# A planned one-core kernel (H3 mixer, then a token-mixing MLP): k by DMA transpose, x statistics from an early copy, tables and silu on GpSimd, PE transposes for three token groups, and an order read from a table

## The chip, the cores and the metric

One NeuronCore of a Trainium2 chip runs the whole program. The metric is device time of one execution in microseconds (us), the median of three runs. Engines: PE (TensorE, the matrix engine; PEld is its weight load), DVE (VectorE), ACT (ScalarE), POOL (GpSimd), SP (SyncE, which issues DMAs). SBUF is the on-chip memory, PSUM the accumulators that PE writes.

## The reference

Everything is bfloat16, sequence S = 2048, width D = 640, F = 1728. `sa ... gb` are six vectors of width D from `silu(c) @ w_mod`.

```python
h = layernorm(x) * (1 + ca) + sa                       # x is A_q
k_shift = sum_t k[s - t] * shift_k[:, t]               # 4 taps, causal
kv = k_shift * v
y  = irfft(rfft(kv, 2S) * rfft(ssm_k, 2S))[:S] + kv * ssm_D      # long convolution along s
x  = x + ga * (h * y)
h  = layernorm(x) * (1 + cb) + sb
t  = gelu(layernorm(h) @ w1)                           # D x D
x1 = h + shift_tokens(t) @ w2                          # four column groups shifted by 1, -1, 2, -2 tokens
x  = x + gb * (x1 + gelu(layernorm(x1) @ w3) @ w4)     # D x F, F x D
```

## The kernel before

**A planner sets the order.** The kernel first lists tasks with `add(engine, cost, function, reads, writes, prio)`: each is a few instructions for one engine, or for whichever of two engines would end earlier. `Planner.run` then plays the list through with the written costs, the dependencies that follow from the named SBUF regions, and four PSUM slots; among ready tasks of an engine the smaller `prio` goes first. The instructions are emitted in the order of the planned starts. On the chip each engine works through its own queue in that order, and semaphores hold an instruction until its inputs are there; a DMA waits likewise in SP's or POOL's queue.

**Stages.** The long convolution is a transform of length 4096 done with matrix products.

- Tables. Sines for the products are made on the chip: POOL writes integer ramps (`iota`, L312), DVE turns them into angles (two `tensor_scalar`, L323 and L324, on 512 columns), ACT takes the sine (L331). `Gs` in RG serves the forward transform, `Hs` in RH the inverse, `F1bd` the first stage.
- Loads. `ssm_k` goes to Ra, two pieces issued by SP and three by POOL. k goes to R3 as it lies (`ktok`, L255, issued by POOL) and is turned with k_transpose: 80 PE transposes into PSUM and twelve copies into kT (in R5). v is turned on the way by four DMA transposes issued by SP (L258) into vT (in R5).
- Forward transform of ssm_k: DVE 32x32 block transposes from Ra to Rb (L386, each behind a one-column add L442), `stage1` on PE (L399) with casts of PSUM into T01 by ACT or DVE (L229, L231), `stage2` on PE (L418) with casts into R3. Between them `k_shift` (L474, PE) with DVE's product with v (L480).
- Forward transform of kv: transposes into Ra (`kvL`), the same two stages, results in R5 (`XS`). Six `mod` pieces (L507) make the vectors.
- x is loaded into Ra, now free (L543, four DMAs in token order for the end of the kernel). DVE takes statistics of each of 16 tiles of 128 tokens (`ln1_stats`, L569 and L570), POOL makes scale and bias (`ln1_fin`, L575 to L578; the power is a GpSimd operation), and `make_q` applies them on ACT (L584) and DVE (L588, L589).
- `inverse1`, ten pieces: DVE multiplies the two transforms (L608, and L610 with a copy whose halves are swapped by DMA, L603), PE multiplies by `EA`, `EB` (L619, L620). Then `inverse2` on PE (L648) with casts into `y_all` (Rb).
- The MLP, in eight groups of two tiles: `chain_a` (L707, L710: y times q, added to x), sum of squares on ACT (L699), mean and power on POOL (`ln_finish`, L685 to L694), `chain_b` (L721 to L723: h), again squares and POOL, `chain_c` (L732), a DMA transpose by SP (L734), `mm_w1` (L764, L774; gelu on ACT, L766, L780), `mm_w2` (L819, sum on DVE L827), a third layernorm (L837 on ACT) with a DMA transpose (L839), `mm_w3` (L854, gelu), `mm_w4` (L877), three DVE operations (L883, L888, L889) and the output DMAs (L892).

The transposition of a tile for w1 reads

```python
add("DVE", 0.42, lambda e, hn=hn, A=A, i=i: nc.vector.tensor_scalar(hn, h_all[:, A, :], rn[0][:, i:i + 1], rn[1][:, i:i + 1], ALU.mult, ALU.add),
    r=[hk_(A), rn[2]], w=[hk], prio=prio)
add("SP", 1.25, lambda e, hn=hn, i=i: nc.sync.dma_start_transpose(hT[:, :, i * P:(i + 1) * P], hn), r=[hk], w=[hTk + ("t",)], prio=prio, lat=1.6)
```

Of the kernel before, what the change touches and what calls it, by code (L numbers as in the profile page):

```python
# [8 lines left out]
BF = mybir.dt.bfloat16  # L9
F32 = mybir.dt.float32  # L10
# [28 lines left out]
class Planner:  # L41
# [3 lines left out]
    SEM = {"PE": 0.22, "ACT": 0.12, "DVE": 0.10, "POOL": 0.15, "SP": 0.0}  # L45
# [44 lines left out]
    def run(self):  # L90
# [4 lines left out]
        order = []  # L95

# [11 lines left out]
        while todo:  # L108
# [49 lines left out]
def kernel(  # L158
# [34 lines left out]
    ident = modv[:, 4, 0:P]  # L193
# [6 lines left out]
    ktok = R3[:, 10240:20480].rearrange("p (t d) -> p t d", d=D)  # L200
# [15 lines left out]
    def ca(n):  # L216
        return 0.12 + 0.00083 * n

    def cd(n):
        return 0.08 + 0.00105 * n  # L220

    def dma(eng, kb, fn, r=(), w=(), prio=None):
        q = nc.sync if eng == "SP" else nc.gpsimd
        return add(eng, 0.55 if eng == "SP" else 1.0, lambda e, q=q, fn=fn: fn(q), r, w, prio, lat=2.0 + kb / 280.0)
# [25 lines left out]
    for b in range(ND):  # L250
        add("SP" if b < 2 else "POOL", 1.5 if b < 2 else 1.0, lambda e, b=b: (nc.sync if b < 2 else nc.gpsimd).dma_start(sT[:, b, :], A_ssm_k[b * P:(b + 1) * P, :]),
            w=[("Ra", 2048 * b, 2048 * b + 2048)], lat=3.5 + 1.5 * b)
    dma("POOL", 8, lambda q: q.dma_start(skT[:], A_shift_k.rearrange("(b p) j -> p b j", p=P)), w=[("skT", 0, 1)])
    for sc in range(4):
        add("POOL", 1.0, lambda e, sc=sc: nc.gpsimd.dma_start(ktok[:, 4 * sc:4 * sc + 4, :], k_flat[512 * sc:512 * sc + 512, :].rearrange("(t p) d -> p t d", p=P)),  # L255
            w=[("R3", 10240 + 2560 * sc, 12800 + 2560 * sc)], lat=9.0 + 2.5 * sc)
    for sc in range(4):
        add("SP", 5.8, lambda e, sc=sc: nc.sync.dma_start_transpose(vT[:, :, sc * 512:(sc + 1) * 512], v_flat[sc * 512:(sc + 1) * 512, :]),  # L258
            w=[("vT", 5 * sc, 5 * sc + 5)], lat=1.5)
# [10 lines left out]
    s64 = mem.tile([P, 1], F32, name="s64")  # L270
    pci = mem.tile([P, 2], I32, name="pci")
# [12 lines left out]
    add("POOL", 0.3, lambda e: nc.gpsimd.memset(F1bd[:], 0.0), w=[("F1", 0, 1)], prio=-2)  # L284
    add("POOL", 0.6, lambda e: make_identity(nc, ident), w=[("modB", 5, 6)], prio=5)

    def f(e):
# [4 lines left out]
        nc.vector.tensor_copy(s64[:], pci[:, 1:2])  # L292
    add("DVE", 0.7, f, r=[("pidx", 0, 1)], w=[("scol", 0, 1)], prio=-2)

    gcol = mem.tile([P, 2, 4], F32, name="gcol")
    hcol = mem.tile([P, 2, 4], F32, name="hcol")
    ci = mem.tile([P, 4], I32, name="ci")

    def f(e):
        nc.gpsimd.iota(ci[:], pattern=[[16, 4]], base=0, channel_multiplier=0)  # L300
    add("POOL", 0.2, f, w=[("ci", 0, 1)], prio=-3)

    def f(e):
        for col, s_ in ((gcol, s64), (hcol, s32o)):
            nc.vector.tensor_scalar(col[:, 0, :], ci[:], s_[:], None, ALU.mult)
            nc.vector.tensor_scalar(col[:, 1, :], ci[:], s_[:], 2048.0, ALU.mult, ALU.add)
    add("DVE", 0.5, f, r=[("ci", 0, 1), ("scol", 0, 1)], w=[("cols", 0, 1)], prio=-1)
    tmp = {"R3": R3[:].bitcast(I32), "RK": RK[:].bitcast(I32)}

    def itab(reg, o, n, pattern, base, prio):  # L310
        ti = tmp[reg][:, o:o + n]
        add("POOL", 0.2 + 0.0012 * n, lambda e: nc.gpsimd.iota(ti, pattern=pattern, base=base, channel_multiplier=0),  # L312
            w=[(reg, 2 * o, 2 * o + 2 * n)], prio=prio)
        return ti, (reg, 2 * o, 2 * o + 2 * n)

    def angles(it, reg, o, s_col, cs_col, ss_col, q, prio):
        ti, tk = it
        n = ti.shape[1]
        ms, ma = (tmp[reg][:, o + n * i:o + n * (i + 1)] for i in range(2))
        keys = [(reg, 2 * o + 2 * n * i, 2 * o + 2 * n * (i + 1)) for i in range(2)]  # L320
        for m_, k_, col in ((ms, keys[0], ss_col), (ma, keys[1], cs_col)):
            def f(e, m_=m_, col=col):
                nc.vector.tensor_scalar(m_, ti, s_col, col, ALU.mult, ALU.add)  # L323
                nc.vector.tensor_single_scalar(m_, m_, q - 1, ALU.bitwise_and)  # L324
            add("DVE", 0.2 + 0.0013 * n, f, r=[tk, ("cols", 0, 1), ("scol", 0, 1)], w=[k_], prio=prio)
        return ms, ma, keys

    def sin_to(dst, ms, q, n, r, w, prio, neg=False):
        b = (b_neg if neg else b_pos)[dst.start_partition():dst.start_partition() + dst.shape[0], :]
        sc = (2.0 if neg else -2.0) * PI_LO / q  # L330
        add("ACT", 0.2 + 0.00098 * n, lambda e: nc.scalar.activation(dst, ms, ACT.Sin, scale=sc, bias=b),  # L331
            r=[r, ("consts", 0, 1)], w=[w], prio=prio)

    it = itab("R3", 4608, 32, [[2, 32]], 1, -2)
    ms, ma, ky = angles(it, "R3", 4640, s32[:], 32.0, 0.0, 128, -1)
    for q in range(4):
        sl = slice(32 * q, 32 * q + 32)
        sin_to(F1bd[sl, q, 0, :], ma[sl, :], 128, 32, ky[1], ("F1", 0, 1, "f"), -1)
        sin_to(F1bd[sl, q, 1, :], ms[sl, :], 128, 32, ky[0], ("F1", 0, 1, "f"), -1, True)
    it = itab("R3", 0, 512, [[2, 8], [128, 64]], 1, -1)  # L340
    for kb in range(4):
        ms, ma, ky = angles(it, "R3", 512 + 1024 * kb, s64[:], gcol[:, 1, kb:kb + 1], gcol[:, 0, kb:kb + 1], 8192, -1)
        k2s = slice(8 * kb, 8 * kb + 8)
        ms3, ma3 = (t.rearrange("p (a b) -> p a b", a=8) for t in (ms, ma))
        wk = ("RG", 2048 * kb, 2048 * kb + 2048, "g")
        sin_to(Gs[:, k2s, 0, 0, :], ma3, 8192, 512, ky[1], wk, 0)
        sin_to(Gs[:, k2s, 0, 1, :], ms3, 8192, 512, ky[0], wk, 0, True)
        sin_to(Gs[:, k2s, 1, 0, :], ms3, 8192, 512, ky[0], wk, 0)
        sin_to(Gs[:, k2s, 1, 1, :], ma3, 8192, 512, ky[1], wk, 0)
# [5 lines left out]
    it = itab("RK", 1536, 64, [[1, 64]], 0, 8)  # L355
    ms, ma, ky = angles(it, "RK", 1600, s64[:], 16.0, 0.0, 64, 30)
# [127 lines left out]
    for j in range(12):  # L484
        k_transpose(j, 20 + (j - 2) / 3.0)
# [483 lines left out]
```

## Time and profile before

| | |
|---|---|
| median of three runs | 370.57 us (369.43 to 371.05) |
| profiled execution | 368.94 us, of which 367.2 from its first to its last instruction (the span) |
| mean granted PE clock in it | 0.916 of full |
| moved by DMA | 35.08 MB |

The profile is one execution. Its lines give for a group of instructions: source line, engine, operation, output<-input, count, then busy us and mean ns of one, then the idle time of the engine just before them and what ended it. Buffer names drop their numbers, so R is R3 or R5 and T is T01. In lines by stretch, each engine's busy us stands with its instruction count in brackets, then the granted PE clock, the DMA share and GB/s. Lines of the chain that ended last give start, length and what. SPq is SP issuing a DMA.

### The profile page before, as it was taken

Reading aid. Unit: us, or ns where it says so; the run is one execution under the profiler, and the core shown is the slowest. Engines: PE = TensorE matmul, PEld = TensorE weight load, DVE = VectorE, ACT = ScalarE, POOL = GpSimd, SP = SyncE. Lnnn points to the kernel's source line nnn. Section 1 sums busy time; section 2 is a strip of 40 time slices with the busy share of each in tenths; the row PEclk is TensorE's granted clock in tenths of the full one; section 3 lists DMA queues with packets and bytes.
Section 4 is the critical chain, followed back from the end, with each engine's and each line's share of the span. In section 5 each row is a group of like instructions: output and inputs, shape, how many; then the busy total and the mean of one; then the engine's idle time right before and its main releaser. Section 6 shows DMA issues by size and latency. Waiting matters only on the chain.

```text
span 367.2 us, 7656 instructions
## 1 busy us (share of the span) xinstructions
PE 290.1 (79%) x3086; PEld 213.8 (58%) x3092; DVE 234.7 (64%) x436; ACT 226.8 (62%) x362; POOL 80.1 (22%) x201
## 2 busy tenths in 40 slices
PE   0459789899834787501686999999999999999993
PEld 0336445577524776401554887786776776768672
DVE  8999999889089899988789786532313031211313
ACT  6959886679905588887789897693471412213020
POOL 8300000000020001485587573341130000000000
PEclk9989999999985799555868999999999999999997
DMA  7999404085962580079012505205010212101001
GB/s 217 339 199 234 142 0 116 2 266 108 215 206 67 133 203 4 4 290 267 3 36 54 91 15 108 61 0 83 26 38 20 54 29 45 38 10 29 18 21 36
DMA packets 49060, 35.08 MB, mean 96 GB/s; under 512 B 35008, under 2 KB 45952, under 8 KB 49024
## 3 DMA queue, kind: packets, MB, share of 16 engines
q1 hardware_dynamic: 47984, 30.39, 34.8%
q0 software_dynamic: 1040, 4.20, 3.4%
q8 instruction: 24, 0.39, 0.4%
q14 instruction: 12, 0.10, 0.1%
HBM read 18.85 MB, written 2.62 MB: 58 GB/s over the span
## 4 chain that ended last, share of the span: by engine, by line
PE 55%; DVE 25%; DMA 8%; ACT 4%; issue 3%; POOL 3%; SPq 1%; DVEq 0%; POOLq 0%; ACTq 0%
PE ps_w L877 18%; PE ps_w L854 18%; PE ps_w L819 6%; PE ps_w L764 5%; DMA Ra<-in_A_q_dram 4%; DVE ln_st L569 3%; DVE Rb L386 3%; DVE R L480 2%; DVE Rb L610 2%; DVE Ra L386 2%; ACT T L229 2%; PE ps_ksh L474 2%; DMA R<-RK 2%; PE ps_s L399 2%; DVE T L231 2%
## 5 line engine op out<-in xcount | busy, mean ns | idle before, releaser
L854 PE MATMUL ps_w<-R,T 128*128 128x256 bf16 (+1 forms) x560 | 66.3, 277 | 2.6 <-DMA R<-RH 2.6
L883 DVE TENSOR_TENSOR T<-ps_w,R 128x640 bf16<-128x640 f32 x16 | 13.2, 825 | 86.3 <-PE ps_w L877 86.3
L877 PE MATMUL ps_w<-T,R 128*128 128x320 bf16 x448 | 68.1, 300 | 0.0
L859 ACT ACTIVATE R<-ps_w 128x1024 bf16<-128x1024 f32 x24 | 24.5, 1022 | 61.7 <-PE ps_w L854 61.6
L854 PEld LDWEIGHTS <-T 128*128 128x128 bf16 (+1 forms) x560 | 54.5, 100 | 13.2 <-issue 6.0
L877 PEld LDWEIGHTS <-R 128*128 128x128 bf16 x448 | 41.7, 97 | 25.6 <-issue 8.4
L229 ACT CAST R<-ps_s 128x640 bf16<-128x640 f32 x49 | 31.4, 744 | 3.2 <-PE ps_s L418 3.2
L764 PE MATMUL ps_w<-R,RG 128*128 128x256 bf16 x160 | 20.4, 287 | 16.3 <-DMA R<-RK 16.3
L619 PE MATMUL ps_i<-EA,Rb 128*128 128x128 bf16 x160 | 23.2, 243 | 11.4 <-DVE Rb L608 11.4
L819 PE MATMUL ps_w<-RG,R 128*128 128x320 bf16 x160 | 25.7, 317 | 5.5 <-ACT R L780 4.1
L699 ACT ACTIVATE RG<-R 128x640 bf16<-128x640 bf16 x32 | 23.5, 736 | 9.9 <-DVE R L827 7.3
L229 ACT CAST T<-ps_s 128x1024 bf16<-128x1024 f32 x25 | 23.7, 1020 | 7.3 <-PE ps_s L399 7.3
L399 PE MATMUL ps_s<-F1bd,Rb 128*128 128x256 bf16 x80 | 13.3, 337 | 18.7 <-DVE Ra L442 14.3
L764 PEld LDWEIGHTS <-RG 128*128 128x128 bf16 x160 | 16.4, 103 | 19.7 <-issue 16.6
L418 PE MATMUL ps_s<-T,RG 64*128 64x160 bf16 x512 | 24.4, 230 | 2.8 <-ACT R L229 0.5
L620 PE MATMUL ps_i<-EB,Rb 128*128 128x128 bf16 x160 | 23.0, 243 | 3.7 <-DVE Rb L610 3.7
L229 ACT CAST T<-ps_i 128x1024 bf16<-128x1024 f32 x20 | 19.6, 1014 | 10.1 <-PE ps_i L620 6.5
L619 PEld LDWEIGHTS <-Rb 128*128 128x128 bf16 x160 | 17.8, 111 | 11.9 <-DVE Rb L608 11.9
L418 PEld LDWEIGHTS <-RG 64*128 64x128 bf16 x512 | 18.1, 94 | 10.9 <-issue 10.2
L819 PEld LDWEIGHTS <-R 128*128 128x128 bf16 x160 | 15.9, 103 | 13.6 <-ACT R L780 4.8
L399 PEld LDWEIGHTS <-Rb 128*128 128x128 bf16 x80 | 9.5, 120 | 22.2 <-DVE Ra L442 14.3
L620 PEld LDWEIGHTS <-Rb 128*128 128x128 bf16 x160 | 17.6, 111 | 5.0 <-DVE Rb L610 5.0
(123 smaller groups left out, 529.5 us busy)
## 6 DMA issues: line engine op xcount, KB each, us to landing
Rb<-in_w_mod_dram SPq DMA_DIRECT2D x6, 800.0 KB, 6.1
RK<-R SPq DMA_DIRECT2D x12, 256.0 KB, 3.8
R<-in_A_k_dram POOLq DMA_DIRECT2D x4, 640.0 KB, 13.5
Ra<-in_A_q_dram SPq DMA_DIRECT2D x4, 640.0 KB, 9.7
out_dram<-RH SPq DMA_DIRECT2D x64, 40.0 KB, 1.6
T<-in_B_w_dram SPq DMA_DIRECT2D x1, 2160.0 KB, 8.2
T<-in_B_w_dram SPq DMA_DIRECT2D x1, 2080.0 KB, 13.9
Rb<-R SPq DMA_DIRECT2D x8, 256.0 KB, 3.7
```

Of the source, the lines that this page charges most:

```text
L229: nc.scalar.copy(dst, src(ps.tile))
L386: add("DVE", 1.95, lambda e: nc.vector.transpose(out=o, in_=i), r=skeys, w=[(dkey, 2048 * b, 2048 * b + 2048)], prio=prio)
L399: nc.tensor.matmul(psv[:, ml, :], lhsT=xL[:, s0:s0 + P], rhs=F1r, start=True, stop=True)
L418: nc.tensor.matmul(psv[:, g, kl, :], lhsT=Gs[64 * g:64 * g + 64, k0 + kl, cc, :, :].rearrange("p o n -> p (o n)"), rhs=T1h[h][64 * g:64 * ...
L619: nc.tensor.matmul(psv[:, w, :], lhsT=TA[:, o:o + P], rhs=EAf, start=True, stop=False)
L620: nc.tensor.matmul(psv[:, w, :], lhsT=TB[:, o:o + P], rhs=EBf, start=False, stop=True)
L699: add("ACT", 0.83, lambda e: nc.scalar.activation(junk, src, ACT.Square, scale=float(D) ** -0.5, accum_out=stat[:, li, 1, t:t + 1]), r=[sk ...
L764: nc.tensor.matmul(pt[:, fb, :], lhsT=w1_sb[:, b, 160 * fb:160 * fb + P], rhs=hT[:, b, :], start=(b == 0), stop=(b == ND - 1))
L819: nc.tensor.matmul(pt[:, hf, 0:320], lhsT=gsf[:, fb, c0:c0 + P], rhs=w2_sb[:, fb, 320 * hf:320 * hf + 320], start=(fb == 0), stop=(fb == 4))
L854: nc.tensor.matmul(pt[:fw, fl, :], lhsT=w3_sb[:, b, fb * P:fb * P + fw], rhs=xT[:, b, :], start=(b == 0), stop=(b == ND - 1))
L859: nc.scalar.activation(g3[g % 2][:, f0:f0 + fn, :], ps.tile[:, 0:fn, :], ACT.Gelu_apprx_tanh)
L877: nc.tensor.matmul(pt[:, hf, 0:320], lhsT=g3[g % 2][:fw, fb, i * P:(i + 1) * P], rhs=w4_sb[:fw, fb, 320 * hf:320 * hf + 320], start=(fb == ...
```

## The change

Statement by statement, with line numbers of the new file:

- k is no longer loaded as it lies. SP issues four more DMA transposes, of k into kT (L294), in turn with those of v; `ktok`, the PE transposes and their twelve copies are gone. All of ssm_k is issued by SP.
- x is loaded twice (L581, eight DMAs): an early copy into Ra between the two uses of Ra as transposed input, from which all 16 tiles' statistics are taken (L592, L593) with one `ln1_fin`; and the copy for the rest, as before.
- Of the sixteen angle computations for `Gs` and `Hs`, four stay on DVE (L341, L342); twelve are three POOL operations each on 512 columns (L355 to L357), with the sine taken by ACT from fractions of a turn. One quarter of `Gs` is copied by POOL (L401) instead of computed twice. `F1bd` is filled by two POOL selects. silu(c) is made of POOL powers, so ACT loads no silu table.
- For the first three of the eight groups (`pe_tr`) the two tile transposes go over PE (L795) and PSUM with a copy by ACT or DVE (L801, L803); the other five stay DMA transposes (L788).
- The layernorm applications (`norm`) may go to ACT (L636) or DVE (L638).
- w3 and w4 are padded to 14 x 128 rows with zeros (POOL memsets), so the last gelu is one instruction.
- The planner's costs are rewritten, DMA transfers share one modelled wire, and `prio` is replaced by `RANK`, a table of 1025 numbers, one for each task.

```diff
+RANK = """
+391 395 588 106 492 422 455 385 608 471 561 869 770 650 781 874 702 438 260 219 446 424 679 880 142 510 467 279 127 53 413 680 212 429 825 542 452 503
...
+        rank = RANK.split()
+        if rank:
+            for t in self.tasks:
+                t.prio = (int(rank[t.no]), t.no)
...
-    for sc in range(4):
-        add("SP", 5.8, lambda e, sc=sc: nc.sync.dma_start_transpose(vT[:, :, sc * 512:(sc + 1) * 512], v_flat[sc * 512:(sc + 1) * 512, :]),
-            w=[("vT", 5 * sc, 5 * sc + 5)], lat=1.5)
+        for dst, off, src, key in ((kT, 16, k_flat, "kT"), (vT, 0, v_flat, "vT")):
+            add("SP", 3.3, lambda e, sc=sc, dst=dst, off=off, src=src: nc.sync.dma_start_transpose(dst[:, :, off + sc * 512:off + sc * 512 + 512], src[sc * 512:(sc + 1) * 512, :]),
+                w=[(key, 5 * sc, 5 * sc + 5)], kb=655, rate=200.0)
...
+    def angles_pool(reg, o, n, pattern, base, s_col, prio, mul=1.0):
...
+        for off in (0.0, 0.25):
+            def f(e, off=off):
+                nc.gpsimd.tensor_scalar(xs, ti, s_col, off, ALU.mult, ALU.add)
+                nc.gpsimd.tensor_scalar(xr, xs, MAGIC, MAGIC, ALU.add, ALU.subtract)
+                nc.gpsimd.tensor_tensor(xs, xs, xr, ALU.subtract)
+            add("POOL", 0.6 + 0.0068 * n, f, r=[keys[0], ("scol", 0, 1)], w=keys[1:], prio=prio)
+            yield xs, keys[1]
...
-    sl_t = add("ACT", 1.6, lambda e: nc.scalar.activation(silu_c[:], c_col[:], ACT.Silu), r=[("ccol", 0, 1)], w=[("siluc", 0, 1)], prio=35, after=[last_sin])
+        nc.gpsimd.tensor_tensor(silu_c[:], ebase[:, 0, :], silu_c[:], ALU.pow)
...
+    x_load(38)
+    for A in range(NT):
+        ln1_stats(A, 39)
+    ln1_fin(0, NT, 39)
...
-    for A in range(6):
-        ln1_stats(A, 66)
-    ln1_fin(0, 6, 66)
...
+    pe_tr = (0, 1, 2)
+
+    def turn(dT, dk, src, sk, i, g, prio):
+
+        if g not in pe_tr:
+            add("SP", 1.3, lambda e: nc.sync.dma_start_transpose(dT[:, :, i * P:(i + 1) * P], src), r=[sk], w=[dk + ("t",)], prio=prio, lat=1.6)
+            return
...
+            for b in range(ND):
+                nc.tensor.transpose(pt[:, 0, b, :], src[:, b * P:(b + 1) * P], ident)
+        t0 = add("PE", 0.4, f, r=[sk, ("RG", 7680, 7808)], alloc=ps, prio=prio)
...
-            t0 = add("PE", 4.0, f, r=[gk3, ("T01", 10240, 10240 + NF * D)], alloc=ps, prio=prio)
+            t0 = add("PE", 3.82, f, r=[gk3, ("T01", 10240, 10240 + NF * D)], alloc=ps, prio=prio)
```

**DVE around the x statistics.** Before, the last of them ahead of the first inverse product (L608) stand behind all casts of the forward transform:

```order
L569 BN_STATS ln_st<-Ra 128x6 x2
L570 BN_AGGR mv_93<-ln_st 128x2
L520 TENSOR_SCALAR modv<-ps_mod 128x640
L608 TENSOR_TENSOR Rb<-R_68,R_67 128x4x16x32
L522 CAST modv<-ps_mod 128x640
L524 CAST modv<-ps_mod 128x640
```

In the new order the first of them follows the casts of ssm_k's first stage (L270 is the cast, L524 the product of shifted k and v):

```order
L270 CAST T_66<-ps_s_455 128x64x4x4
L270 CAST T_66<-ps_s_474 128x64x4x4
L524 TENSOR_TENSOR R_68<-ps_ksh,R_68 128x512
L270 CAST R_67<-ps_s_496 128x320x2
L592 BN_STATS ln_st<-Ra 128x6 x2
L593 BN_AGGR mv_93<-ln_st 128x2
```

and the first product (L664) now follows a cast directly, with casts of kv's second half behind it:

```order
L270 CAST R_68<-ps_s_1288 128x320x2
L270 CAST R_68<-ps_s_1306 128x320x2
L664 TENSOR_TENSOR Rb<-R_68,R_67 128x4x16x32
L270 CAST R_68<-ps_s_1351 128x320x2
L664 TENSOR_TENSOR Rb<-R_68,R_67 128x4x16x32
L666 TENSOR_TENSOR Rb<-R_68,Rb 128x4x16x32
```

The statistics moved ahead by some sixty rows.

**SP at the start.** Before, its queue up to the x load (L543) held two of the five ssm_k pieces and the four transposes of v:

```order
L247 DMA Dcol<-in_A_ssm_D_dram 128x5x1
L251 DMA Ra<-in_A_ssm_k_dram 128x2048 x2
L258 DMA_TRANSPOSE R_68<-in_A_v_dram 128x5x512 x4
L247 DMA c_col<-in_c_dram 128x5x1
L497 DMA Rb<-in_w_mod_dram 128x5x640 x3
L603 DMA RK<-R_67 64x2048 x4
L497 DMA Rb<-in_w_mod_dram 128x5x640 x3
L543 DMA Ra<-in_A_q_dram 32x16x640 x4
```

Now it reads, from its first DMA:

```order
L290 DMA Ra<-in_A_ssm_k_dram 128x2048
L294 DMA_TRANSPOSE R_68<-in_A_k_dram 128x5x512
L286 DMA Dcol<-in_A_ssm_D_dram 128x5x1
L290 DMA Ra<-in_A_ssm_k_dram 128x2048 x2
L294 DMA_TRANSPOSE R_68<-in_A_k_dram 128x5x512
L290 DMA Ra<-in_A_ssm_k_dram 128x2048
L294 DMA_TRANSPOSE R_68<-in_A_v_dram 128x5x512
L290 DMA Ra<-in_A_ssm_k_dram 128x2048
L294 DMA_TRANSPOSE R_68<-in_A_v_dram 128x5x512
L294 DMA_TRANSPOSE R_68<-in_A_k_dram 128x5x512
L294 DMA_TRANSPOSE R_68<-in_A_v_dram 128x5x512
L581 DMA Ra<-in_A_q_dram 32x16x640 x4
```

The early x copy stands behind six of the eight transposes and all of ssm_k; two transposes and the w_mod loads follow it.

**DVE at the first token groups.** Before, the applied layernorms ahead of w1 (L732) go to the SP transpose, and the queue continues with q:

```order
L589 TENSOR_TENSOR RQ<-RQ,modv 128x640
L732 TENSOR_SCALAR RK<-R_68,ln_rs,ln_nb 128x640 x2
L588 TENSOR_TENSOR RQ<-RQ,modv 128x640
L589 TENSOR_TENSOR RQ<-RQ,modv 128x640
L707 TENSOR_TENSOR R_68<-Rb,RQ 128x8x5x16
```

Now the copies of PE's transposes (L803) stand in the queue behind them (L638):

```order
L761 TENSOR_TENSOR R_68<-Rb,RQ 128x8x5x16 x2
L764 SCALAR_TENSOR_TENSOR Ra,stat<-R_68,Ra 128x640 x2
L638 TENSOR_SCALAR RK<-R_68,ln_rs,ln_nb 128x640 x2
L761 TENSOR_TENSOR R_68<-Rb,RQ 128x8x5x16
L803 COPY R_67<-ps_tr 128x5x128
L764 SCALAR_TENSOR_TENSOR Ra,stat<-R_68,Ra 128x640
L803 COPY R_67<-ps_tr 128x5x128
```

A new kind of row, the PSUM copy, moved in between two products of the next group.

More of the change, by code (lines that the diff above doesn't have):

```diff
@@ L270 @@
     s64 = mem.tile([P, 1], F32, name="s64")
+    s64t = mem.tile([P, 1], F32, name="s64t")
     pci = mem.tile([P, 2], I32, name="pci")
@@ L292, in f @@
         nc.vector.tensor_copy(s64[:], pci[:, 1:2])
+        nc.vector.tensor_scalar_mul(s32o[:], s32o[:], 1.0 / 8192)
+        nc.vector.tensor_scalar_mul(s64t[:], s64[:], 1.0 / 8192)
     add("DVE", 0.7, f, r=[("pidx", 0, 1)], w=[("scol", 0, 1)], prio=-2)
[L295 to L301, printed above, removed]
```

303 lines of the change are left out of this document (160 added, 143 removed), and 26 rows, old and new, of the table RANK.

## Prediction

> **What bounds the kernel now.** I read the page's busy shares and its slices first, then the busy time by stage, then the chain that ended last, then what VectorE waited for.
>
> ```profile
> PE 290.1 (79%) x3086; PEld 213.8 (58%) x3092; DVE 234.7 (64%) x436; ACT 226.8 (62%) x362; POOL 80.1 (22%) x201
> ...
> DVE  8999999889089899988789786532313031211313
> ...
> PEclk9989999999985799555868999999999999999997
> ```
>
> No engine is full over the whole span, but the slices show two halves: VectorE (DVE) is at 8 or 9 tenths for the first half, and from about 200 us the clock row stays at 9. The stretches below are cut where the inverse transform starts, where the first layernorm chain starts, and where the w3 products start.
>
> ```profile
> core 0: us, PE busy (x) PEld busy (x) DVE busy (x) ACT busy (x) POOL busy (x), PEclk, DMA share, GB/s
> 0.00:110.70 110.70, 78.20 (x886) 53.13 (x892) 93.54 (x151) 83.72 (x122) 13.78 (x27) 0.97 0.66 169
> 110.70:148.30 37.60, 25.79 (x496) 23.95 (x506) 35.68 (x55) 26.62 (x29) 2.40 (x14) 0.82 0.40 99
> 148.30:199.30 51.00, 23.99 (x466) 16.87 (x465) 44.10 (x108) 42.27 (x81) 33.43 (x75) 0.67 0.40 114
> 199.30:361.50 162.20, 162.12 (x1253) 119.81 (x1253) 59.58 (x125) 74.23 (x132) 30.55 (x86) 0.99 0.20 41
> ```
>
> So the end is: the moment w3 starts (199.3), plus 162.2 us in which PE never rests, plus 5.7 us of last outputs. Before 199.3 DVE works 93.5 of 110.7, 35.7 of 37.6 and 44.1 of 51.0 us. A gain has to come from stages A, B and C ahead of 199.3, and there from DVE's work or its waits. The chain and DVE's waits name the large ones.
>
> ```profile
> 87.74 14.13 DMA Ra<-in_A_q_dram
> ...
> 140.12 1.22 DVE Rb L610
> ...
> 148.34 0.37 DVE R L707
> ...
> 159.44 0.34 POOL rs L575
> ...
> 162.10 0.82 POOL nb L578
> ...
> 166.48 6.43 DMA R<-RK
> ...
> 196.53 2.60 DMA R<-RH
> ...
> 199.27 0.80 PE ps_w L854 x4
> ```
>
> ```profile
> DVE ln_st L569 <- DMA Ra<-in_A_q_dram: 9.7, 1, 9.7
> DVE RK L732 <- POOL ln_nb L694: 4.3, 3, 2.5
> ```
>
> The x load holds the chain for 14.13 us and DVE for 9.7. The last product of the inverse ends at 141.34, and 7.0 us pass until its results reach L707. The layernorm chain then carries two transposes by DMA (6.43 and 2.60) and a statistics finish on POOL (159.44 to 162.92).
>
> **The change, stage A (to the first product L664, 110.7 now).** Rows that price DVE's instructions:
>
> ```profile
> L323 DVE TENSOR_SCALAR R<-R,s,gcol 128x512 int32<-128x512 int32 x8 | 5.4, 676 | 0.0
> L324 DVE TENSOR_SCALAR R<-R 128x512 int32<-128x512 int32 x8 | 4.1, 511 | 0.3
> L323 DVE TENSOR_SCALAR RK<-RK,s32o,hcol 128x512 int32<-128x512 int32 x8 | 4.3, 539 | 0.0
> L324 DVE TENSOR_SCALAR RK<-RK 128x512 int32<-128x512 int32 x8 | 3.4, 427 | 0.3
> L231 DVE CAST T<-ps_s 128x1024 bf16<-128x1024 f32 x15 | 17.5, 1214 | 1.2 <-PE ps_s L399 1.1
> L231 DVE CAST R<-ps_s 128x640 bf16<-128x640 f32 x15 | 11.7, 816 | 0.1
> L231 DVE COPY R<-ps_kT 128x1024 bf16<-128x1024 bf16 x1 | 0.7, 680 | 0.0
> L231 DVE COPY R<-ps_kT 128x512 bf16<-128x512 bf16 x1 | 0.4, 406 | 0.0
> L569 DVE BATCH_NORM_STATS2 ln_st<-Ra 128x6 f32<-128x320 bf16 x32 | 13.5, 463 | 9.7 <-DMA Ra<-in_A_q_dram 9.7
> L570 DVE BATCH_NORM_AGGREGATE mv<-ln_st 128x2 f32<-128x12 f32 x16 | 3.3, 209 | 0.6
> L520 DVE TENSOR_SCALAR modv<-ps_mod 128x640 bf16<-128x640 f32 x1 | 0.8, 771 | 0.0
> L721 DVE TENSOR_SCALAR R<-Ra,ln_rs,ln_nb 128x640 bf16<-128x640 bf16 x16 | 7.1, 444 | 3.0 <-POOL ln_nb L694 2.9
> ```
>
> Counted in the new order up to the first product: tables, 17.2 us before, now four pairs at 0.676 + 0.511 = 4.7 (-12.5). Casts into T, 15 to 9 (-7.3). Casts into R, 15 to 11 (-3.3). The two kT copies go (-1.1). Sixteen x statistics stand here instead of eight (+8 x (2 x 0.463 + 0.209) = +9.1), and six mod pieces instead of four (+1.6). Sum -13.5: DVE's 93.5 becomes 80.0. Its idle 17.2 loses the 9.7 of the x load and keeps 7.5.
>
> ScalarE takes six more T casts but loses ten kT copies and the silu table load, so its 83.7 hardly grows; it stays next to DVE and is the second bound. PE loses the 80 k transposes, which cost nothing on the end, since PE is not the bound here.
>
> The early x copy (into Ra, free between the ssm_k transposes and kvL) is a new wait, since sixteen statistics and everything behind them on DVE stand behind it. On SP it now stands behind five ssm_k loads and six transposes.
>
> ```profile
> L258 SPq DMA_TRANSPOSE R<-in_A_v_dram x4: 3503/4154/16427, 2.3 to 27.2; - x4
> ...
> 2.35 28.37 SPq L258 DMA_TRANSPOSE R<-in_A_v_dram  x4
> ...
> 85.67 2.88 SPq L543 DMA_DIRECT2D Ra<-in_A_q_dram  x4
> ```
>
> One transpose occupies SP for 3.5 to 16.4 us, median 4.15; the 16.4 is the first, with POOL's own loads of k and ssm_k in flight. Those loads now stand in SP's own queue, in order with the transposes, so I take about 4. SP reaches x at 0.8 + 6 x 4 + some 3 for the small issues = 27.7, and x lands 16.2 us after its first issue (85.67 to 101.87): 43.9. DVE has about 35 us of work ahead of the first statistic and some 5 of waits for PE, so it is there at 40: +4. The other bound is a gain: none of it if DVE is itself late.
>
> POOL takes over twelve angle triples, 36 operations on 512 elements, that no row shows, and the price on DVE is the shared waiting.
>
> ```profile
> 14.77 2.47 POOL L350 TENSOR_SCALAR_AFFINE_SELECT RQ<-skT 128x2560 bf16<-128x2560 bf16 x1 [6.17 <-DMA skT<-in_A_shift_k_dram]
> ...
> 16.34 0.91 DVE L442 TENSOR_TENSOR Ra<-Ra,Dcol 128x1 bf16<-128x1 bf16 x1
> ...
> L442 DVE TENSOR_TENSOR Ra<-Ra,Dcol x5: 114/121/914, 12.0 to 21.4; 128x1 bf16<-128x1 bf16 x5
> ...
> L312 POOL IOTA R<- 128x512 int32 x1 | 0.6, 571 | 0.0
> ```
>
> By the 512-element iota one operation is at least 0.57 us, 21 us in all; the affine select, 2.47 for 2560 elements, gives 0.49 for 512. I take twice the iota, 41 us, because an iota reads nothing and these read one stream or two. No row sets the upper end, so I carry the cover as one: the tables Hs are read first by the inverse's second half, near 125 us, and POOL has some 15 us of other work before that, so 36 operations may take (125 - 15) / 36 = 3 us each; beyond that its tables hold the chain. On DVE, one L442 of 0.12 us took 0.91 and ended as POOL's select did, 17.24: a wait of 0.8 behind one POOL instruction. Some 30 small DVE operations (tables, E, L500, the silu copy) run beside the triples: between 0 and 30 x 0.79 = 23.7 us. Nearest are the L323 rows, 0.676 beside POOL's DMA issues and 0.539 later: 8 x 0.11 for the remaining tables plus half a wait for each of five L500 is 2.9. I take +2.9.
>
> [...]
>
> Stage A: 80.0 + 7.5 + 2.9 + 4 = 94.4.
>
> **Stage B (37.6 now).** Twenty products stay. Two mod pieces leave (-1.6), two casts into R come (+1.6), two norms come from ScalarE (+0.9). The seven statistics that filled the 7.0 us gap leave, the gap stays, and some five q multiplies of 0.5 now lie in it (-2.7). The second x copy waits for the last first-stage product on kvL, about 90, and lands 16.2 later at 106; DVE reaches the first norm on it at 103: +3. Together 38.8, so 133.2.
>
> **Stage C (51.0 now).** DMA transposes of 6.43 and 2.60 become PE transposes and a copy; the k transposes show both prices.
>
> ```profile
> 41.74 0.61 PE ps_kT L461 x8
> ...
> 223.44 2.82 PE ps_w L819 x20
> ```
>
> Five cost 0.4, the copy of 640 about 0.5 by the kT copies, with two handovers 1.5 and 1.3: -4.9 and -1.3. The statistics finish leaves the chain (-3.5), and one x statistic (-1.1): 40.2 by the chain. By DVE's queue: up to the copies that w3 waits for, 97 instructions now stand in this stage (accumulator reads counted) where the stage row has 108, since two tiles fewer are carried to the second layernorm, two w2 sums fewer are made, and norms and transpose copies come in. At the row's mean, 44.10 / 108 = 0.408, that is 39.6, and the 5 or so of POOL waits (4.3 in the L732 row) stay: 45. I take 45, since DVE is the bound; the chain's 40 is the lower end. w3 starts at 178.2 instead of 199.3.
>
> **The tail.** 162.2 stays, plus one w2 tile not yet done (2.82 / 2 = 1.4), 20 transposes at 0.076 (1.5), and 2 for waits of PE that a fuller DVE and ScalarE bring: 167.1. End 345.3, span 351.0. The padding of w3 and w4 to 128 rows leaves the number and width of matmuls, so it costs nothing; its memset runs on POOL long before w3. The profiled execution took 368.94 for a span of 367.2, so 352.7; the runs' median, 370.57, stands 1.63 above that execution, so 354.
>
> **Rivals.**
> 1. PE waits in the tail. DVE and ScalarE enter the tail with two tiles more unfinished, and the order was searched with 3.82 us for a w4 tile, which takes 4.12:
>
> ```profile
> 219.32 4.12 PE ps_w L877 x28
> ```
>
> Against it: DVE and ScalarE are busy only 59.6 and 74.2 of 162.2 now, and a PE slower than its plan gives the others time. If each of the five w1 groups still to come is 1.6 late, that is 8 us: 362.
> 2. The front packs better: the 4 and 3 for x, and half of the 7.5 and of the 5, vanish: 341. For it: those waits are spread among fillers that a search may have used.
> 3. The k transposes don't stream. The mean of the four was 28.37 / 4 = 7.1. Six of them put x at 62.5, 18.6 later, with DVE standing: 373, no better than before, and the k and v pieces late as well. It decides at 7 us each. Against it: the median 4.15.
> 4. POOL locks DVE out: 23.7 instead of 2.9, so 375, slower. [...] It decides where the average wait passes 0.7 us over 30 operations. Against it: four of five L442 took 0.12.
>
> **Chances.** Forecast 0.55, tail waits 0.17, better packing 0.18, transposes 0.05, lock 0.05. Half of the packing case lies under 341, and rivals 3 and 4 lie over 364, so 341 to 364 leaves out 0.19. Forecast, tail and packing are all faster by over 0.5% (1.9 us, about what can be told): 0.90. Transposes count 0.04 as same; the rest, 0.06, is slower.
>
> **What would show it.** Right: first product near 94, first L761 near 133, w3 at 178, PE at 9 tenths from there; DVE's wait for x at most 5; 36 POOL operations near 1 us in the first 75 us. Wrong: SP transposes above 6 us; DVE's small operations at 0.5 to 0.9; gaps in PE after w3 starts; ScalarE at 9 tenths ahead of 94 while DVE idles.

## The result, and the profile after

The changed kernel takes 349.45 us (median of 4 runs, 347.12 to 352.81), the kernel before 370.2 beside it (4 runs, 369.43 to 371.05): 0.942 of the time, with a 95% interval of 0.936 to 0.948. One execution of the changed kernel (352.81) and one each of three experiments (1292, 366.2 and 350.89) were slow ones, and the ratios leave them out. The forecast was 354, with a range of 341 to 364. The profiled execution took 347.12 us for a span of 345.4. The total came within 5 us, but two of the four stages did not: errors of opposite sign, +7.1 and -11.1, partly cancelled, so the nearness of the total is in part luck.

Three rows of the page: busy times, VectorE's slices and the granted clock. A slice is now 8.6 us.

```profile
PE 278.5 (81%) x3072; PEld 214.0 (62%) x3072; DVE 222.3 (64%) x426; ACT 205.4 (59%) x326; POOL 128.3 (37%) x241
...
DVE  7996879999891777698889899532023164204232
...
PEclk9996999999999689755999999999999999999997
```

POOL rose from 80 to 128 us. VectorE's high stretch ends near 216 us, but it has a hole at slices 13 to 17 (digits 1, 7, 7, 7, 6), about 103 to 146 us, which the kernel before did not have there; its one slice of 0, at 92 to 101 us, is gone. The same stretches as in the prediction, cut where the same instructions start:

```profile
0.00:95.00 95.00, 68.92 (x701) 44.75 (x703) 83.94 (x138) 66.19 (x94) 65.91 (x70) 0.96 0.75 175
95.00:140.90 45.90, 29.89 (x617) 27.09 (x612) 29.66 (x35) 31.39 (x39) 2.19 (x13) 0.89 0.86 185
140.90:183.20 42.30, 24.60 (x482) 17.71 (x482) 38.15 (x98) 37.79 (x72) 26.82 (x62) 0.76 0.32 107
183.20:339.20 156.00, 155.08 (x1285) 124.46 (x1282) 68.71 (x155) 70.00 (x122) 33.38 (x97) 1.00 0.18 38
```

The columns are as before: length, busy times of PE, PE's weight loads, VectorE, ScalarE and POOL, then granted clock, DMA share and GB/s. Beside the forecast:

| stretch | before | forecast | measured | error |
|---|---|---|---|---|
| A, to the first product L664 | 110.7 | 94.4 | 95.0 | +0.6 |
| B, to the first q product L761 | 37.6 | 38.8 | 45.9 | +7.1 |
| C, to the first w3 product | 51.0 | 45 | 42.3 | -2.7 |
| tail, to PE's end | 162.2 | 167.1 | 156.0 | -11.1 |

With the last outputs that gives 345.4 against a forecast span of 351.0. What needs explaining is why B grew although VectorE has 6 us less work there, and why the tail shrank although PE has 32 matmuls more.

For B, the waits of VectorE, and then rows of the chain that ended last:

```profile
DVE RQ L638 <- DMA Ra<-in_A_q_dram: 7.1, 1, 7.1
...
DVE Rb L666 <- DMA Rb<-R: 3.6, 2, 1.9
...
DVE R L761 <- ACT Rb L268: 2.8, 1, 2.8
DVE Rb L666 <- DMA RK<-R: 2.3, 2, 1.8
```

```profile
99.83 14.43 DMA Rb<-R
...
117.42 7.14 DMA Rb<-R
...
125.93 6.88 DMA Rb<-R
...
237.07 10.92 PE ps_w L930 x100
...
249.89 3.80 PE ps_w L948 x28
```

Rb<-R and RK<-R are the ky copies, the swap of partition halves that the inverse's second multiply L666 reads. Three of them hold the chain for 28 us. In 95 to 141 us they land late:

```profile
Ra<-in_A_q_dram SPq DMA_DIRECT2D x4, 640.0 KB, 11.2
RK<-R SPq DMA_DIRECT2D x8, 256.0 KB, 10.7
Rb<-R SPq DMA_DIRECT2D x6, 256.0 KB, 7.3
```

The last column is the median time to landing; for the kernel before it reads 3.8 (RK) and 3.7 (Rb) for the two kinds of copy over the whole run. For the tail, the last row of the chain stands out: 28 w4 matmuls take 3.80 us, where before they took 4.12.

### The profile page after: what moved, and what is told of

It is laid out like the page before. It is cut to its first block, busy times and chain, and to the rows that moved or that the text cites. A ratio compares the mean times of both kernels' runs of the same rounds, so it can differ in the third digit from the quotient of the medians.

```text
span 345.4 us, 7581 instructions
## 1 busy us (share of the span) xinstructions
PE 278.5 (81%) x3072; PEld 214.0 (62%) x3072; DVE 222.3 (64%) x426; ACT 205.4 (59%) x326; POOL 128.3 (37%) x241
## 3 DMA queue, kind: packets, MB, share of 16 engines
q1 hardware_dynamic: 52832, 35.24, 43.9%
## 4 chain that ended last, share of the span: by engine, by line
PE 41%; SPq 14%; DVE 10%; ACT 10%; POOL 10%; DMA 9%; issue 4%; DVEq 0%; ACTq 0%; POOLq 0%
PE ps_w L948 15%; PE ps_w L930 13%; SPq L294 12%; DMA Rb<-R 8%; ACT T L268 4%; PE ps_w L897 4%; PE ps_w L842 3%; ACT RG L753 2%; ACT Rb L268 2%; POOL ln_rs L747 2%; PE ps_ksh L518 1%; DMA c_col<-in_c_dram 1%; DVE R L905 1%; POOL RK L356 1%; DVE R L777 1%
## 5 line engine op out<-in xcount | busy, mean ns | idle before, releaser
L930 PE MATMUL ps_w<-R,T 128*128 128x256 bf16 x560 | 63.1, 273 | 0.2 <-DVE R L803 0.2
L948 PE MATMUL ps_w<-T,R 128*128 128x320 bf16 x448 | 63.0, 299 | 0.0
L934 ACT ACTIVATE R<-ps_w 128x1024 bf16<-128x1024 f32 (+1 forms) x32 | 29.3, 915 | 51.4 <-PE ps_w L930 50.9
L930 PEld LDWEIGHTS <-T 128*128 128x128 bf16 x560 | 54.7, 98 | 7.2 <-DVE R L803 0.4
L948 PEld LDWEIGHTS <-R 128*128 128x128 bf16 x448 | 43.8, 98 | 16.5
L739 POOL TENSOR_SCALAR ln_nm<-stat 128x2 f32<-128x2 f32 x24 | 8.7, 360 | 85.6 <-DVE R L905 56.5
L268 ACT CAST T<-ps_s 128x1024 bf16<-128x1024 f32 x31 | 29.8, 1033 | 13.4 <-PE ps_s L457 13.1
L753 ACT ACTIVATE RG<-R 128x640 bf16<-128x640 bf16 x32 | 23.5, 735 | 17.1 <-DVE R L905 14.5
L676 PEld LDWEIGHTS <-Rb 128*128 128x128 bf16 x160 | 17.1, 108 | 15.1 <-DVE Rb L666 13.9
L905 DVE SCALAR_TENSOR_TENSOR R<-ps_w,R 128x640 bf16<-128x640 f32 x16 | 13.1, 821 | 18.6 <-PE ps_w L897 18.5
L457 PEld LDWEIGHTS <-Rb 128*128 128x128 bf16 x80 | 8.9, 114 | 23.6 <-DVE Ra L500 16.6
L518 PE MATMUL ps_ksh<-R,RQ 128*128 128x512 bf16 x80 | 20.9, 407 | 3.0 <-DMA R<-in_A_k_dram 1.6
## 6 DMA issues: line engine op xcount, KB each, us to landing
Ra<-in_A_q_dram SPq DMA_DIRECT2D x8, 640.0 KB, 10.7
```

The source lines that it names most:

```text
L268: nc.scalar.copy(dst, src(ps.tile))
L518: nc.tensor.matmul(pt[:, i, :], lhsT=diagw[:, b, jj, :], rhs=kT[:, b, 16 - jj + sc * 512:16 - jj + sc * 512 + 512], start=(jj == 0), stop= ...
L676: nc.tensor.matmul(psv[:, w, :], lhsT=TB[:, o:o + P], rhs=EBf, start=False, stop=True)
L753: add("ACT", 0.79, lambda e: nc.scalar.activation(junk, src, ACT.Square, scale=float(D) ** -0.5, accum_out=stat[:, li, 1, t:t + 1]), r=[sk ...
L930: nc.tensor.matmul(pt[:, fl, :], lhsT=w3_sb[:, b, fb * P:(fb + 1) * P], rhs=xT[:, b, :], start=(b == 0), stop=(b == ND - 1))
L934: nc.scalar.activation(g3[g % 2][:, f0:f0 + fn, :], ps.tile[:, 0:fn, :], ACT.Gelu_apprx_tanh)
```

## Experiments

Times below are medians; ratios are to the kernel before, run on the same chip. First L664, first L761 and first w3 product are read from each profiled execution; where an edit shifts the lines, the same products are meant. The edits are shown shortened.

| run | L664 | L761 | w3 | span | median | ratio (95%) |
|---|---|---|---|---|---|---|
| changed kernel | 95.0 | 140.9 | 183.2 | 345.4 | 349.45 | 0.942 (0.936 to 0.948) |
| without padding | 94.7 | 143.2 | 186.6 | 355.9 | 357.37 | 0.966 (0.960 to 0.972) |
| before, with padding | 112.4 | 150.0 | 202.5 | 360.6 | 361.42 | 0.979 (0.973 to 0.985) |
| no second x copy | 94.1 | 131.5 | 175.0 | 337.0 | 338.69 | 0.919 (0.911 to 0.927) |
| second copy on POOL's queue | 95.1 | 142.1 | 185.6 | 347.8 | 349.28 | 0.946 (0.940 to 0.951) |
| hand priorities | 106.2 | 154.9 | 198.9 | 363.2 | 364.32 | 0.981 (0.974 to 0.989) |
| turns by DMA | 93.9 | 139.6 | 194.2 | 361.2 | 363.46 | 0.983 (0.978 to 0.987) |
| no early x copy | 93.0 | 139.1 | 185.2 | 347.2 | 345.59 | 0.936 (0.930 to 0.942) |
| tables on VectorE | 118.0 | 150.0 | 192.3 | 354.5 | 357.37 | 0.968 (0.962 to 0.974) |
| x cut in two | 93.2 | 137.2 | 180.4 | 343.2 | 345.62 | 0.935 (0.931 to 0.938) |
| and w1, w2 late | 94.4 | 137.2 | 183.3 | 345.4 | 347.72 | 0.940 (0.935 to 0.945) |
| and c early | 107.5 | 141.3 | 185.3 | 347.8 | 349.85 | 0.947 (0.943 to 0.950) |
| x cut, realistic rate | 94.4 | 138.8 | 182.4 | 344.8 | 348.07 | 0.941 (0.936 to 0.947) |

One profiled execution scatters: B, the difference of the first two columns, was 45.7 to 48.5 us in the four runs with no edit in it (the changed kernel, without padding, turns by DMA, no early x copy).

### The padding, both ways

```diff
-lhsT=w3_sb[:, b, fb * P:(fb + 1) * P]      # out pt[:, fl, :]
+fw = min(P, F - fb * P)                    # 64 for the last block
+lhsT=w3_sb[:, b, fb * P:fb * P + fw]       # out pt[:fw, fl, :]
-lhsT=g3[:, fb, ...], rhs=w4_sb[:, fb, ...]
+lhsT=g3[:fw, fb, ...], rhs=w4_sb[:fw, fb, ...]
```

> The changed kernel, with the last block of w3's outputs and of w4's inputs cut back to its 64 real rows, as the kernel before has it; the order on every engine stays. Theory 1 (the padding itself shortened the last phase, which the forecast costed at nothing): the w4 tile of 28 matmuls goes back from 3.80 to 4.12 us (16 tiles: +5.1), eight w3 groups from 7.64 to 7.97 (+2.6), so about +7.7: some 357 us, with the stretch from the first w3 product to the last product near 163.7 instead of 156.0. Rival (the matmuls are shorter for another reason, the order or a higher granted clock): rows stay at 3.80 and 7.64, time within 2 us of 349.5.

The second run has the reverse edit in the kernel before.

> The kernel before, with the padding of w3 and w4 to 128 rows alone; the order on every engine stays, two memsets on POOL come in and eight split gelus become one each. Theory 1: the w4 tile goes from 4.12 to 3.80 us, the w3 group from 7.97 to 7.64, and the time falls by about 7.7 to 362.5. Rival (the order or the clock made them shorter): 4.12 stays, and 370 within 2.

Both moved as theory 1 said: +7.9 and -8.2 by the medians (to be compared with 349.45 and 369.61). In the changed kernel the stretch from w3 to PE's end is 163.1 without the padding and 156.0 with it; the w4 tile is 4.12 without it. The kernel before with padding, and then the changed kernel without it, on the chain:

```profile
220.86 3.80 PE ps_w L872 x28
```

```profile
196.01 4.12 PE ps_w L952 x28
```

So 16 x 0.32 = 5.1 us come from w4, and the other 2, by difference, from w3. Where it sits is seen by form in the groups of weight loads of the kernel before, whose last number is idle time in front of them:

```profile
L877 PEld LDWEIGHTS <-R 128*128 128x128 bf16 x416 | 38.7, 98 | 17.1 <-issue 0.2
...
L854 PEld LDWEIGHTS <-T 128*64 128x64 bf16 x40 | 3.7, 109 | 1.7 <-issue 1.7
...
L877 PEld LDWEIGHTS <-R 64*128 64x128 bf16 x32 | 3.0, 93 | 8.4 <-issue 8.2 <-ACT RH L837 0.3
```

32 weight loads of 64 rows had 8.4 us of idle in front of them, 0.26 each, put down to issue; the 416 of 128 rows had 17.1, 0.04 each. The load itself is hardly shorter (93 against 98 ns). Sixty-four rows alone do not bring the gap: the 512 loads of 64 rows in the forward transform (L418) had 10.9 us of idle in front of them, 0.02 each. There all loads of a product have 64 rows, while in w4 the short block stands among full ones; that this is the cause was not tested. The 64-column loads of w3 took 109 ns, more than the full ones' 98 to 100. This row was there to be read before the forecast.

### The second copy of x

```diff
-x_load(45)
+x_load(45, late=True)     # the four DMAs are not issued
```

> The changed kernel without the second copy of x (the q norms and the sums that read x then read what the transposed kv left in its place); nothing else moves. Theory 2 (the second copy, in one queue with the ky copies, lengthened the inverse's first half from the forecast 38.8 to 45.9 us): the ky copies land in 4 to 5 us instead of 7.3, VectorE's 7.1 us wait for x and its 5.9 for ky go, the stretch from the first product to the first q product shortens by 7 to 13, and the total is 337 to 343. Rival (that stretch is set by the queue's total of ky copies and weights, or by PE and ScalarE): under 3 us shorter, 347 or more.

```diff
-dma("SP", 655, ...)       # second copy only
+dma("POOL", 655, ...)
```

> The changed kernel with the second copy of x issued by POOL in its own queue; nothing else moves. If what hurts is the place behind and between the ky copies in one queue: ky lands in 4 to 5 us again, x a few us later than now, total 343 to 347. If it is the bytes, since the 16 DMA engines are busy 0.86 of that stretch: ky stays at 7 or more, x lands no earlier, total 348 to 352.

Without the copy 10.8 us go, 8.5 of them in B: 37.4 instead of 45.9, where the forecast without its +3 was 35.8. In B the RK and Rb copies land in 5.8 and 6.2 us instead of 10.7 and 7.3. VectorE's order is the same in both kernels, so the rows can be set side by side: the norm that reads x, and the multiply behind it that reads a ky copy, in the changed kernel and then without the copy:

```profile
111.92 0.80 DVE L638 TENSOR_SCALAR RQ<-Ra,rs,nb 128x640 bf16<-128x640 bf16 x2 [7.12 <-DMA Ra<-in_A_q_dram]
114.39 1.22 DVE L666 TENSOR_TENSOR Rb<-R,Rb 128x2048 bf16<-128x2048 bf16 x1 [1.67 <-DMA Rb<-R]
```

```profile
103.74 0.80 DVE L638 TENSOR_SCALAR RQ<-Ra,rs,nb 128x640 bf16<-128x640 bf16 x2
104.45 1.22 DVE L666 TENSOR_TENSOR Rb<-R,Rb 128x2048 bf16<-128x2048 bf16 x1
```

The changed kernel is 0.9 behind at the first product, 8.2 at the norm, 9.9 at the multiply and 9.3 at the first q product. So 7.2 of the 8.5 arise at the wait for x and 1.8 at the ky copy behind it; the later ky waits are no longer than without the x copy, where 5.1 us of them are left. Theory 2 holds for the total and for x, but not in its words that the waits for ky go. What x and ky would cost apart this run can't say: the ky copy issued at 99.83 landed at 114.26, and would have held the multiply with x in time too. Moving the copy to POOL's queue changed nothing that can be told: 349.28, and in the stretch the ky copies still took 10.8 and 8.0:

```profile
RK<-R SPq DMA_DIRECT2D x8, 256.0 KB, 10.8
Ra<-in_A_q_dram POOLq DMA_DIRECT2D x3, 640.0 KB, 14.5
Rb<-R SPq DMA_DIRECT2D x6, 256.0 KB, 8.0
```

There VectorE waited 9.5 us for x. So in these runs what makes the ky copies late is the bytes and not the place in the queue. From 95 to 141 us the changed kernel moves 8.5 MB, at a DMA share of 0.86, where the kernel before moves 3.7 MB from 111 to 148, at 0.40.

### The searched order

The table RANK is emptied, and nothing else is edited.

> The changed kernel with the table of searched priorities emptied, so that the priorities written beside each piece of work set the order, as in the kernel before. Theory (the forecast's: the gain is work taken from VectorE ahead of w3, and the order only has to keep it fed): at most 5 us slower, 350 to 355. Rival (the search found most of the gain): w3 starts 10 us or more later, 360 or more, with VectorE idle longer ahead of the first product of the inverse.

The rival is right: 364.32, 14.9 slower. w3 starts at 198.9, where the kernel before has 199.3. With hand priorities the edits ahead of w3 together brought nothing there, and the 5.9 us that are left of the gain are no more than what the padding gives. The sums up to the first q product, here and for the changed kernel, name the difference:

```profile
sum 154.90, PE 103.20 PEld 73.84 DVE 127.86 ACT 88.66 POOL 67.97; mean PE 51.60 PEld 36.92 DVE 63.93 ACT 44.33 POOL 33.99
```

```profile
sum 140.90, PE 98.81 PEld 71.84 DVE 113.60 ACT 97.57 POOL 68.09; mean PE 49.40 PEld 35.92 DVE 56.80 ACT 48.79 POOL 34.05
```

VectorE has 14.3 us more to do, ScalarE 8.9 less. By form, VectorE makes 40 casts out of PSUM with hand priorities (14 into T, 26 into R) and 22 in the changed kernel (9 and 13). In this comparison the searched order differs in which engine empties which bank. What a search for the hand priorities' own weights would reach was not tried.

### Turns of token groups on PE or by DMA

```diff
-pe_tr = (0, 1, 2)
+pe_tr = ()
```

A task that issues nothing keeps the numbering of the table.

> The changed kernel with all turns of token groups by DMA, none on PE. The forecast's terms: -4.9 and -1.3 ahead of w3 are lost, 1.5 us of PE work is saved: +4.7, so 354, w3 starting about 6 later. Rival (the turns were hidden behind VectorE's queue in that stretch, which the forecast took as the bound): under 2 us.

14.0 slower, three times the forecast's term: 11 ahead of w3 and the rest behind. The turns waited twice in a row on the chain:

```profile
159.02 8.48 DMA R<-RK
...
168.97 5.86 DMA R<-RK
```

and SP's queue shows what they stood behind, the loads of w3 and w4:

```profile
158.51 0.40 SPq L977 DMA_DIRECT2D T<-in_B_w_dram  x1
159.02 1.93 SPq L788 DMA_TRANSPOSE R<-RK  x1
161.04 0.54 SPq L979 DMA_DIRECT2D T<-in_B_w_dram  x1
161.63 0.58 SPq L978 DMA_DIRECT2D T<-in_B_w_dram  x1
163.32 5.55 SPq L788 DMA_TRANSPOSE R<-RK  x1
```

PE waited 18.5 us for these turns at the first w1 products. The two waits are 14.3 us. Since the priorities were searched with PE turns, some of the 14 may be the misfit of the order, these waits included: another order could put the loads elsewhere, and none was searched.

### The early copy of x

```diff
-x_load(38)
+x_load(38, late=True)     # the four DMAs are not issued
```

> The changed kernel without the early copy of x; the statistics then read what is left in its place, and are as long as ever. The forecast priced the early copy at +4 of waiting on VectorE; the trace shows 1.3 waited there. Theory 1 (that wait is all it costs): 1 to 4 less, 345.5 to 348.5. Theory 2 (the first stage is bound by its loads, 175 GB/s, and the copy's 2.56 MB delay the k and v pieces behind it and c): up to 14.6 less, the first product near 85 and the total 337 to 342.

345.59, or 3.9 less, at the end of theory 1's range and far from theory 2's; the two intervals overlap (0.930 to 0.942 and 0.936 to 0.948), so the size is not settled. The first product comes at 93.0, just ahead of the 93.2 to 95.1 of the runs that keep the copy. The profiled execution was the longest of the four, and its w3 starts later than the changed kernel's; the median goes the other way, so I don't place the rest by stage. The first stage is not bound by this copy's 2.56 MB.

### Tables on VectorE or on POOL

```diff
-nc.gpsimd.tensor_scalar(xs, ti, s_col, off, ALU.mult, ALU.add)
-nc.gpsimd.tensor_scalar(xr, xs, MAGIC, MAGIC, ALU.add, ALU.subtract)
-nc.gpsimd.tensor_tensor(xs, xs, xr, ALU.subtract)
+nc.vector.tensor_scalar(m, ti, s_col, off, ALU.mult, ALU.add)   # integers
+nc.vector.tensor_single_scalar(m, m, 8191, ALU.bitwise_and)
```

> The changed kernel with the tables of the second stage and of the inverse's second half made by VectorE again (two integer operations each, sines with a bias), in place of the twelve triples on POOL; the order shifts where the planner places them. The forecast's terms: +12.5 of VectorE work ahead of the first product (some less, 12 x 1.0 for the twelve), -2.9 of waiting for POOL: about +9, 357 to 360. Rival 4 (POOL's lock is dear): VectorE's waits for POOL vanish and pay for it, under 3 slower. Rival (loads or PE bound the first stage, not VectorE): also under 3, but with VectorE's idle time ahead of the first product falling by about 10.

357.37, or 7.9 slower. The sum to the first q product:

```profile
sum 150.00, PE 98.65 PEld 71.22 DVE 123.08 ACT 98.42 POOL 22.54; mean PE 49.33 PEld 35.61 DVE 61.54 ACT 49.21 POOL 11.27
```

VectorE has 9.5 us more and that point comes 9.1 later, against about 9 in the forecast's terms. That the first product moves by 23 and B shrinks to 32 is the planner's order: it put more of the work ahead of the first product (99.6 of VectorE instead of 83.9). POOL's 45.5 us are hidden.

### Attempts at a better version

Tiles 5 to 15 of the second copy go behind the last ky copies; then w1 and w2 too; then c early.

```diff
-x_load(45)                                        # all of x
+dma("SP", ..., x_all[32*cg:32*cg+32, 0:5, :])     # here
+dma("SP", ..., x_all[32*cg:32*cg+32, 5:16, :], after=last_ky_copies)
```

> The changed kernel with the second copy of x cut in two: tiles 0 to 4, which the first five q need, at the place where it stands now, and tiles 5 to 15 behind the last ky copies. Nothing is left out. Theory (the bytes moved while ky and the first q wait are what costs): 11/16 of the copy, 1.8 MB, leave the stretch, which is worth 11/16 of what leaving out the whole copy was worth (10.8): about 7, so 342 to 344, with VectorE's 7.1 us wait for x down to 2 or so. Rival (the later part is then late for the q of tile 5 and on): 347 or more, with waits for x behind the first q product.

> The same, and the loads of w1 and w2 (1.6 MB) put behind the second part of x as well. Theory: another 1.6 MB leave the stretch; ky copies then land in 4 to 5 us and the total is 339 to 342. Rival: VectorE and ScalarE bound the stretch once x is out, as in the run without the second copy (37.5 us), so nothing more comes: within 1.5 us of the run with x cut alone; or w1 comes late for the first w1 product, near 150, and it is slower.

> The same as the last, and the small load of c issued next to that of D at the start instead of behind the k and v transposes, so that silu on POOL need not wait until 53 us; the order shifts a little where the planner uses that. Theory (c's late landing held POOL's tables and the modulation): 2 to 4 less than without it. Rival (POOL has slack there, 65.9 busy of 95): within 1.

The cut gives 345.62, about 3.8 less than the changed kernel and half of what was expected; the two intervals overlap a little (0.931 to 0.938 and 0.936 to 0.948), so the size is not settled. The ky copies, from 90 to 150 us, land as in the kernel before:

```profile
RK<-R SPq DMA_DIRECT2D x12, 256.0 KB, 4.0
...
Rb<-R SPq DMA_DIRECT2D x6, 256.0 KB, 4.1
```

and the wait for x fell from 7.1 to 3.1, but other waits came:

```profile
DVE R L770 <- ACT Rb L271: 5.2, 1, 5.2
DVE RQ L643 <- DMA Ra<-in_A_q_dram: 3.1, 1, 3.1
DVE Rb L669 <- PE ps_i L680: 3.0, 2, 2.3
```

The planner now believed that x comes early, and put q work ahead of multiplies. Moving w1 and w2 as well gained nothing (347.72, 2.1 more than with x cut alone): the theory is out, and the rival's "within 1.5" is the nearer. With c early it was 2 more again (349.85), which neither its theory nor its rival expected: the planner's order changed with it, and the first product came at 107.5. So c's late landing can't be priced by that run.

> The kernel with x cut in two, with the planner told that the first part of the copy comes at 110 KB a us instead of 330: in the run with the cut, 800 KB took from 92.5 to 101.0, 94 KB a us. The planner then places the ky copies and their multiplies ahead of the first q. Theory (what is left over the 37.5 us of the run without the copy is VectorE's queue standing behind a q that waits for x, 3.1 us, and multiplies that come later for it): 341 to 343.5, with no wait for x over 1 us in the stretch. Rival (the stretch is bound by the chain copy, multiply, free buffer over three ky buffers): 345 or more.

348.07: the wait for x is gone, but 4.8 us of waits for PE and 3.4 for ky copies stand in its place. The rival fits better, though I can't tell it from an order that needs a new search. What holds B at 43 to 44 us, with x mostly out of the way and the ky copies on time, against 37.4 without x, stays open; the order is another one as well. The version with x cut is, by its median, the fastest here that computes everything.

## Why the prediction was right, step by step

**Stage A was right for its size.** The forecast was 80.0 of VectorE work, 2.9 of waits for POOL and 11.5 of idle; measured are 83.94, which holds both, and 11.06. The terms for tables, net of the wait for POOL, hold (run with tables on VectorE: 9.5 by work, 9.1 by time). The terms for casts, -7.3 and -3.3, hold too, but I booked them to the change's parts, and the run with hand priorities shows that they belong to the searched order.

**POOL's price was a little low, and covered.** The three operations of a triple:

```profile
14.82 0.70 POOL L355 TENSOR_SCALAR R<-R,s64t 128x512 f32<-128x512 int32 x1 [2.80 <-ACT RG L363]
15.61 1.93 POOL L356 TENSOR_SCALAR R<-R 128x512 f32<-128x512 f32 x1
17.62 1.28 POOL L357 TENSOR_TENSOR R<-R 128x512 f32<-128x512 f32 x1
```

Twelve triples are 12 x 3.91 = 47 us, where I took 41 and bounded them at 3 us an operation.

**VectorE's wait behind POOL was right in size and partly wrong in source.** Over the first 13 us VectorE's small table operations took some 5 us more than their undisturbed like. The worst does not come from the triples:

```profile
9.69 2.39 DVE L342 TENSOR_SCALAR RK<-RK 128x64 int32<-128x64 int32 x1
```

The same operation on 64 elements took 0.20 at 5.60. It ended at 12.08, as a select on POOL did (12.02) that the kernel before has too:

```profile
9.56 2.46 POOL L402 TENSOR_SCALAR_AFFINE_SELECT RQ<-skT 128x2560 bf16<-128x2560 bf16 x1
```

In the run with tables on VectorE the same operation still takes 2.38, and the small ones together some 4 us more than undisturbed. So the triples brought only about 1 of the 5. Only one of the twelve ran in these 13 us, though. Beside the others stand few small operations (five L500 took 1.1 us in all), and of the large ones the 32 statistics show nothing: their mean is 465 ns, against 463 before. The rival that priced this wait in full, 375, is out.

**The early copy was over-priced as a wait.** SP reached x at 29.6 (forecast 27.7), its first statistic ran at 45.8 (x forecast to land at 43.9), and VectorE waited 1.3 instead of 4. The rival of slow transposes is out: the first six occupied SP for 25 us together, 4.2 each, though the one behind x took 13.16:

```profile
26.52 2.87 SPq L294 DMA_TRANSPOSE R<-in_A_v_dram  x1
29.57 3.07 SPq L581 DMA_DIRECT2D Ra<-in_A_q_dram  x4
32.68 13.16 SPq L294 DMA_TRANSPOSE R<-in_A_v_dram  x1
```

**Stage B failed at one step: "+3" for the second x copy.** The term measured 8.5 in the stage and 10.8 in the total. I let x be issued at 90 and land at 106, with VectorE there at 103. SP issued it from 94.4, behind four ky issues (91.5 to 94.3) and the last first-stage product on kvL, which ended at 93.3 and not near 90; the norm that reads x started 17.5 later, at 111.9, where I took 16.2; VectorE had been there since 104.8. So the wait itself was 7.1. And I did not ask what else is in flight beside x: the ky copies are, and the one that the next multiply reads landed only at 114.3. That they alone make the rest is not shown, since with x cut they land as before and B is still 44.0. The row that would have told me is the DMA share: 0.40 in that stage before, with 2.6 MB to be added and weights moving in.

**Stage C was 2.7 better than taken.** I took 45 by VectorE's queue and kept the chain's 40.2 as the lower end; 42.3 lies between. VectorE's 98 instructions took 38.15, against 97 and 39.6. The term for the turns (-4.9 and -1.3) was low for this order: undoing them costs 14, since without them the turns stand behind w3's and w4's loads twice in a row.

**The tail failed at the sentence on padding.** "The padding of w3 and w4 to 128 rows leaves the number and width of matmuls, so it costs nothing" counted instructions and did not look at the gaps between them: it gains 7.1 in the profiled runs and 7.9 to 8.2 in the medians. Of the 2 us for waits of PE 0.8 were seen, by the list of its waits. Of the 3 that remain of the 11.1, some 1.7 (17 matmuls at 4.0 / 39 us) stood in the 162.2 that I carried over: in the first 4.0 us of that stretch, 199.3 to 203.3, the granted clock was 0.57 and PE did 22 matmuls, where the changed kernel has 1.00 and 39 (183.2 to 187.2). The kernel before with padding does its first 60 there in 6.71 us, against 8.38 without padding, and its tail is 152.4, or 9.8 shorter and not 7.1. The last 1 stays open. So the rival of tail waits is out, and the better-packing rival as well: the total fell towards it for another reason.

## What to carry to other kernels

Price a moved transfer by when its queue can issue it and by what else is on the wire in its new place: the stage's DMA share, and whose small copies hold its chain (here 8.5 us in the stage, where +3 was taken). Read the idle time in front of weight loads by form (0.26 against 0.04 us here) before calling a change of tile shape free. When an order has been searched, give it a term of its own, since each edit is worth only what the order makes of it: undoing the search cost 14.9 us, as much as undoing the dearest edit, 14.0.

## What the runs showed of the hardware

- Weight loads of 64 rows, on w4's last block, had 0.26 us of idle in front of each, against 0.04 for 128 rows, and against 0.02 for the 64-row loads of the forward transform; padding with zeros took 0.32 us off a tile of 28 matmuls.
- On POOL a 512-element operation with two constants took 1.93 us, one with a column and a constant 0.70, and a difference of two tensors 1.28. A power of 16 elements a partition was dearer than any of them:

```profile
76.99 2.93 POOL L599 TENSOR_TENSOR rs<-rs,mhalf 128x16 f32<-128x16 f32 x1
```

- ScalarE loaded a table three times in the kernel before and twice in the changed one, 1.28 us each.
- A DMA transpose of a token tile, 2.6 us to landing by the changed kernel's median, took 5.9 and 8.5 beside 4.2 MB of weights in its queue.
- The first product moved between 93.2 and 95.1 us over eight profiled runs with no edit ahead of it, and B between 45.7 and 48.5 over four, so a stage's difference of 2 us or less, and of 3 in B, says little here.
